# Strip 0 of 576 tokens, batch 1's x by token, and other places for the loads of batches 1, 2 and 3

## The chip, the cores and the metric

The kernel runs on one core of a Trainium2 chip. The metric is the device time of one execution in microseconds (us), as the median of several runs. One further execution was recorded by the hardware profiler; times of single steps below are from that one, counted from the start of its span.

The engines have short names in the profile: PE is TensorE (PEld is its weight load), DVE is VectorE, ACT is ScalarE, POOL is GpSimd, SP is SyncE. L161 is line 161 of the kernel.

## The reference

Linear attention with a norm over each head, and then a bilinear feed-forward layer:

```python
# q, k, v: (8 batches, 8 heads, 576 tokens, 64)
kv = np.einsum('bhsd,bhse->bhde', k, v)
out = np.einsum('bhsd,bhde->bhse', q, kv)
rms = np.sqrt(np.mean(out * out, axis=-1, keepdims=True) + 1e-06)
attn = out / rms * g_norm
# x: (8 * 576 = 4608 tokens, 8 * 64 = 512)
x = attn.transpose(0, 2, 1, 3).reshape(4608, 512)
a = x @ w_a          # 512 -> 1536
b = x @ w_b          # 512 -> 1536
y = (a * b) @ w_out  # 1536 -> 512, float32
```

## The kernel before

All products are taken in bf16 and summed in PSUM, which has eight banks of 512 fp32 columns. `xt` holds x transposed (features on partitions, four chunks of 128, and 4608 tokens along the columns).

**Strips.** The feed-forward layer goes over the tokens in nine strips of 512. In a strip, a `Unit` takes one chunk `fc` of 128 of the 1536 hidden features: four products with `wa_t` (L371), a copy to SBUF by ACT (L373), four products with `wb_t`, and a multiplication by DVE into `abt` (L377). After twelve units follow four output groups (`ffn_o`, L434) of 128 tokens: twelve products with `wo_t` each (`o_mm`), a copy out of PSUM by DVE or ACT in turn (`o_out`, L429 and L431) into one of four buffers `o_sb`, and a store by SP. All matrix products of the layer are issued by `product` (L159 to L161), which splits each into two halves of 64 weight columns when `halves[0]` is set; the halves run side by side.

**Batches.** x of a batch has to be there before the strip that holds its tokens. Batch 0 has 576 tokens, so strip 0 lies within it; strip 1 (tokens 512 to 1023) needs batch 1 as well. Batches 0 and 1 (`EARLY`) have their q, k, v loaded by pairs of heads (`load_pair`, L123), and q is transposed by TensorE (`qtr`). x is made by pair: `px` or `x` (L253, with the block-diagonal `kvb`), then products with `ones` (`pss`) to sum the squares, and `pst` (L240). For batch 1 these steps lie between the pieces of strip 0's output groups (L575 to L591).

From batch 2 on, q goes through DRAM: `load_late(b)` (L136) issues on POOL two DMAs of q into `qs_d[b]` and four of k and v (`ktl`, `vtl`, with two buffers each), and `transpose_q(b)` (L153) has SP transpose it into `qT[b % 2]`. From batch 3 on, a small POOL copy from the other `qT` buffer stands ahead of the issues, so that POOL waits there until the batch before is transposed. `kv` (L170) makes k^T v of all heads. Then x is made by token in five chunks (four of 128 tokens and one of 64): `tx` (L286) multiplies qT and kv into banks 4 to 7, the bank `lent` and bank `O` = 3; ACT squares (`tsq`), DVE sums (`tss`), ACT takes the reciprocal root and POOL multiplies it with g (`trs`), DVE scales to bf16 in `x_tok`, and SP transposes that into `xt` (`txt`).

**Order.** The schedule is by hand: every engine runs its instructions in the order of the program text. In the loop over strips 1 to 7 (L632) each strip has slots n = 0 to 15, twelve units and four output groups. `slot(A, s, n)` (L601) says what of batch s + 1 is done after which unit or group: `k0` is the slot of k^T v, `x0` that of `tx`, and the steps of the chunks follow at distances from `x0`. A half slot lies in the middle of a unit or group. Where `transpose_q` and `load_late` stand is at L644 to L649.

**Loads at the start.** POOL issues, in this order: batch 0's pairs, the weights `wa_t` and `wb_t` in slices of 256 columns (two `fc`), the twelve rows of `wo_t`, batch 1's pairs, and `load_late(2)`.

Of the kernel before, what the change touches and what calls it, by code (L numbers as in the profile page):

```python
# [15 lines left out]
def kernel(  # L16
# [28 lines left out]

    pool = ctx.enter_context(tc.tile_pool(name="sb", bufs=1))
# [21 lines left out]
    kvs = [sb([128, NP, D], BF16, f"kvs{i}") for i in range(2)]  # L68

    kvb = sb([128, NP, 128], BF16, "kvb")  # L70
    xt = sb([128, KC, n_tok], BF16, "xt")
    abt = [[sb([128, STRIP], BF16, f"ab{i}_{f}") for f in range(FC)] for i in range(2)]
# [36 lines left out]
    O = 3  # L109
# [26 lines left out]
    def load_late(b):  # L136
        if b > EARLY:

            nc.gpsimd.tensor_copy(gate, qT[(b - 1) % 2][0:1, 0, 0:1])  # L139
        d = qs_d[b].rearrange("t (h d) -> t h d", h=H)  # L140
        for hs in (slice(0, NP), slice(NP, H)):
            nc.gpsimd.dma_start(out=d[:, hs, :], in_=q[b, hs].rearrange("h t d -> t h d"))  # L142
        n = 128 * LC
        for t, src in ((ktl[b % 2], k), (vtl[b % 2], v)):
            nc.gpsimd.dma_start(  # L145
                out=t[:, :, 0:LC, :],
                in_=src[b, :, 0:n].rearrange("h (t c) d -> t h c d", c=LC),
            )
            nc.gpsimd.dma_start(
                out=t[0 : S - n, :, LC, :], in_=src[b, :, n:].rearrange("h t d -> t h d")  # L150
            )
# [12 lines left out]
    class Attn:  # L164
# [20 lines left out]

        def kv_out(self, ps, src):
            for j in range(2):
                r = slice(j * D, (j + 1) * D)
                nc.scalar.copy(kvb[r, ps, r], src[r])
# [63 lines left out]
        def x(self, p, i0):  # L253
            for h in range(2):
                product(
                    P[:, i0 + h, 0:HF],
                    kvb[:, p, :],
                    self.qT[:, p, h * HF : (h + 1) * HF],
                    start=True,
                    stop=True,  # L260
                )


# [22 lines left out]
        def tx(self, lent):  # L286
            self.lent = lent
            for c in range(LC + 1):
                t0, _ = self.rows(c)
                for p in range(NP):  # L290
                    for j, (i, c0) in enumerate(self.place(c)):
                        r = slice(j * D, (j + 1) * D)
                        nc.tensor.matmul(  # L293
                            P[:, i, c0 + p * D : c0 + (p + 1) * D],
                            lhsT=self.qT[r, p, t0 : t0 + 128],
                            rhs=self.kvs[r, p, :],
                            start=True,
                            stop=True,
                        )


            _, r = self.rows(LC)
            for j, (i, _) in enumerate(self.place(LC)):
                nc.scalar.copy(
                    x_last[r, j], P[r, i, 0 : STRIP // 2].rearrange("t (p d) -> t p d", p=NP)
                )
# [13 lines left out]
        def trs(self, c):  # L320
            _, r = self.rows(c)
            n = r.stop - r.start
# [7 lines left out]
            nc.gpsimd.tensor_mul(  # L330
# [17 lines left out]
    class Unit:  # L348
        n = 0

        def __init__(self, s, fc, a, b):
            self.s, self.fc, self.a, self.b = s, fc, P[:, a, :], P[:, b, :]
            self.t = a_sb[Unit.n % 4]
            Unit.n += 1

        def mm(self, w, kcs):
            t0 = self.s * STRIP
            for kc in kcs:
                product(
                    self.a if w is wa_t else self.b,  # L360
                    w[:, kc, self.fc * 128 : (self.fc + 1) * 128],
                    xt[:, kc, t0 : t0 + STRIP],
                    start=(kc == KORD[0]),
                    stop=(kc == KORD[-1]),
                )
# [5 lines left out]
        def part_a(self, kcs=KORD):  # L371
            self.mm(wa_t, kcs)
            nc.scalar.copy(self.t, self.a)  # L373

        def part_b(self, kcs=KORD):
            self.mm(wb_t, kcs)
            nc.vector.tensor_mul(abt[self.s % 2][self.fc], self.b, self.t)  # L377

        def rest(self, kcs=KORD):
            self.part_a(kcs)  # L380
            self.part_b(kcs)
# [7 lines left out]
    def ffn_ab(s, fc, between=None):  # L389
# [4 lines left out]
        u.b = P[:, ab_bank(), :]  # L394
# [19 lines left out]
    def o_mm(s, g, i, fcs, e0=0, e1=d_model):  # L414
        for fc in fcs:
            product(
                P[:, i, e0:e1],
                abt[s % 2][fc][:, g * 128 : (g + 1) * 128],
# [48 lines left out]
    nc.vector.memset(kvb, 0.0)  # L467
# [10 lines left out]
    for i in range(1, d_ff // WC):  # L478
        load_ab(i * WC, (i + 1) * WC)
    for i in range(FC):  # L480
        load_o(i)
    for p in range(NP):
        load_pair(1, p)
    load_late(2)
# [70 lines left out]
    u1.part_b((2, 3))  # L555

# [6 lines left out]
    for fc in range(4, FC):  # L563
        ffn_ab(0, fc)
# [3 lines left out]
    h1, h2 = range(0, FC // 2), range(FC // 2, FC)  # L568

    nc.sync.dma_start(out=gate_d, in_=vt[1][0:1, H - 1, EC - 1, D - 1 : D])  # L570
    nc.sync.dma_start(out=g_all, in_=g_norm.partition_broadcast(128))
    transpose_q(2)
    ffn_o(0, 0, X[0])
    pieces = [(1, h1), (1, h2), (2, h1), (2, h2), (3, h1), (3, h2)]
    for n, (g, fcs) in enumerate(pieces):  # L575

        halves[0] = n > 0
        o_mm(0, g, O, fcs)
        if fcs is h2:
            o_out(0, g, O)  # L580
        if 0 <= n - 2 < NP:
            A.pss(n - 2, SS)
            A.pst(n - 2, X[n % 2])
        if 0 <= n - 1 < NP:
            A.x(n - 1, X[(n - 1) % 2])
            A.psq(n - 1, X[(n - 1) % 2])
        if n < NP:
            A.qtr(n, 2)
            A.kv1(n, 2)
            A.kv_out(n, P[:, 2, STRIP - D :])  # L590
            A.qtr_out(n, 2)  # L591
    u0 = Unit(1, 0, 2, 3)
    u1 = Unit(1, 1, 4, 5)
    u0.first((0, 1, 2))
    u1.first((0, 1, 2))
    u0.rest((3,))
    u1.rest((3,))
# [3 lines left out]
    def slot(A, s, n):  # L601

        kb = P[:, 7, :].rearrange("q (b p e) -> q b p e", b=2, e=D)
        if s == 1:
            k0, xs = 5, (6.5, 8, 9.5, 11, 12.5)
        else:
            k0, x0 = {2: (2, 3.5), 3: (4, 5.5), 4: (0, 1.5), 5: (4, 5.5), 6: (0, 1.5)}[s]
            xs = tuple(x0 + x for x in (0, 1.5, 2.5, 4, 5))

        k0, x0 = {1: (5, 6.5), 2: (1, 2.5), 3: (4, 5.5), 4: (0, 0.5), 5: (4, 5.5), 6: (0, 0.5)}[s]  # L610
# [9 lines left out]
        if m == 0:  # L620
            A.tx(ab_bank())
        for c in range(LC + 1):
            if m == 1.5 * c:
                A.tsq(c)
            if m == (1, 2, 4, 5, 7)[c]:
                A.tss(c)
            if m == (1, 2, 4, 5, 7)[c] + 0.5:
                A.trs(c)
            if m == (1, 2, 4, 5, 7)[c] + 1.5:
                A.txt(c)  # L630

    for s in range(1, N_STRIP - 1):  # L632
        b = s + 1
        A = Attn(b) if b < B else None
        for n in range(FC + 4):
# [5 lines left out]
            if A:  # L641
                slot(A, s, n)

            if s == 1 and n == 3:  # L644
                load_late(3)
            if b + 1 < B and n == (12, 4, 8, 5, 8)[s - 1]:
                transpose_q(b + 1)
            if b + 2 < B and n == (14, 10, 14, 8)[s - 1]:
                load_late(b + 2)  # L649
# [47 lines left out]
```

## Time and profile before

| | us |
|---|---|
| median of 3 runs | 312.36 |
| lowest and highest | 312.31, 312.39 |
| the profiled execution's own time | 312.61 |
| its span | 310.8 |
| strip 0's first product to its first output product | 14.1 to 35.15 |
| strip 0's output groups with batch 1's attention | 35.15 to 49.96 |
| strip 1, units and output groups | 49.96 to 82.75 |
| one `load_late`, issue of batch 3's six DMAs on POOL | 62.39 to 68.79 |

The times of the stages are read from TensorE's and POOL's timelines: a start time, a duration, the engine and line, the operation with what it writes and reads, and how often. The span is what the profiler saw of the core; the 1.8 us around it belong to the execution's time. TensorE's clock was granted in full (1.00) over the whole span. The groups by line and form give, per instruction, 691 ns for DVE's product of 128x512, 586 ns for ACT's copy of the same size, about 680 ns for DVE's sums and scalings by token, 1046 ns for POOL's product by token, and about 2.6 us from issue to landing for SP's transpose of a chunk of x.

### The profile page before, as it was taken

How to read it: one execution, taken by the hardware profiler on the slowest of the kernel's cores; microseconds unless marked ns; L12 is line 12 of the kernel's file. 1: busy time of each engine (PE TensorE's matmuls, PEld its weight loads, DVE VectorE, ACT ScalarE, POOL GpSimd, SP SyncE). 2: the span in 40 equal slices, each digit the busy share in tenths (PEclk: the TensorE clock that was granted, in tenths of full speed). 3: DMA queues.
4: the chain of work that ended last, by engine and by line, in shares of the span. 5: the costliest groups of instructions: out<-in, count | busy, mean ns of one | idle time of the engine just before them, and what ended most of it. 6: DMA issues, size and time to landing. Idle time of an engine off the chain costs nothing.

```text
span 310.8 us, 6542 instructions
## 1 busy us (share of the span) xinstructions
PE 304.3 (98%) x2684; PEld 157.6 (51%) x2701; DVE 140.6 (45%) x235; ACT 117.0 (38%) x231; POOL 101.3 (33%) x123
## 2 busy tenths in 40 slices
PE   7899999999999999999999999999999999999996
PEld 3444476655555555555555555444444444444444
DVE  4544335458248603484386123752782143214321
ACT  3743255354255313551564034632651233123310
POOL 8954991093274630043646300221240000000000
PEclk9999999999999999999999999999999999999999
DMA  8999999999899999047998990073021200030002
GB/s 180 197 196 199 201 188 168 161 169 184 174 137 185 139 174 193 2 84 134 178 177 118 162 188 2 19 160 110 20 51 42 103 1 0 34 103 0 0 36 101
DMA packets 94403, 36.29 MB, mean 117 GB/s; under 512 B 64934, under 2 KB 89894, under 8 KB 94374
## 3 DMA queue, kind: packets, MB, share of 16 engines
q0 software_dynamic: 59120, 18.44, 56.6%
q1 hardware_dynamic: 34786, 16.93, 25.0%
q10 hardware_dynamic: 468, 0.51, 0.6%
q8 instruction: 21, 0.34, 0.5%
q14 instruction: 8, 0.07, 0.1%
HBM read 37.78 MB, written 12.98 MB: 163 GB/s over the span
## 4 chain that ended last, share of the span: by engine, by line
PE 79%; DMA 12%; POOL 7%; issue 1%; ACT 0%; POOLq 0%
PE P L161 77%; DMA wb_t<-in_moe_w_b_dram 6%; DMA vtl<-in_v_dram 4%; DMA wo_t<-in_moe_w_out_dram 2%; PE P L293 1%; PE P L178 1%; POOL vt L119 1%; POOL qt L119 1%; POOL qs L142 1%; POOL kt L119 1%; POOL wa_t L477 0%; POOL wb_t L477 0%; POOL wo_t L134 0%; POOL ktl L145 0%; POOL vtl L145 0%
## 5 line engine op out<-in xcount | busy, mean ns | idle before, releaser
L377 DVE TENSOR_TENSOR ab<-P,asb 128x512 bf16<-128x512 f32 x108 | 74.4, 691 | 103.2 <-PE P L161 99.9
L161 PE MATMUL P<-xt,wb_t 128*64 128x512 bf16 (+1 forms) x641 | 111.4, 379 | 0.2
L161 PE MATMUL P<-xt,wa_t 128*64 128x512 bf16 (+1 forms) x636 | 111.0, 379 | 0.6 <-issue 0.2
L373 ACT CAST asb<-P 128x512 bf16<-128x512 f32 x108 | 63.1, 586 | 89.6 <-PE P L161 89.5
L161 PE MATMUL P<-wo_t,ab 128*64 128x512 bf16 (+3 forms) x673 | 95.5, 371 | 0.3
L161 PEld LDWEIGHTS <-ab 128*64 128x64 bf16 (+1 forms) x678 | 47.5, 106 | 45.0
L161 PEld LDWEIGHTS <-wa_t 128*64 128x64 bf16 (+1 forms) x644 | 46.0, 106 | 46.2 <-issue 0.6
L161 PEld LDWEIGHTS <-wb_t 128*64 128x64 bf16 (+1 forms) x644 | 45.8, 106 | 45.8
L330 POOL TENSOR_TENSOR sqt<-rst,g_all 128x512 f32<-128x512 f32 (+1 forms) x24 | 25.0, 1046 | 83.0 <-ACT rst L323 83.0
L429 ACT COPY osb<-P 128x512 f32<-128x512 f32 x17 | 10.0, 586 | 70.2 <-PE P L161 60.2
L431 DVE COPY osb<-P 128x512 f32<-128x512 f32 x18 | 12.4, 691 | 44.9 <-PE P L161 40.4
L142 POOL DMA_DIRECT2D qs<-in_q_dram x12 | 19.8, 1654 | 0.7 <-issue 0.3
L314 DVE TENSOR_REDUCE sst<-sqt 128x8 f32<-128x512 f32 (+1 forms) x24 | 16.3, 680 | 1.7 <-ACT sqt L310 1.5
L339 DVE TENSOR_TENSOR qv<-P,sqt 128x512 bf16<-128x512 f32 x18 | 12.3, 681 | 0.0
L330 POOL TENSOR_TENSOR k_x<-rst,g_all 128x512 f32<-128x512 f32 x6 | 6.3, 1044 | 17.4 <-ACT rst L323 17.4
L323 ACT ACTIVATE rst<-sst,eps_t 128x8 f32<-128x8 f32 (+1 forms) x30 | 9.0, 300 | 7.2 <-DVE sst L314 7.0
L310 ACT ACTIVATE sqt<-P 128x512 f32<-128x512 f32 x18 | 10.5, 585 | 0.1
L243 DVE SCALAR_TENSOR_TENSOR xt<-P,g_col,rs 128x288 bf16<-128x288 f32 x16 | 7.5, 511 | 5.1 <-ACT rs L233 5.1
L134 POOL DMA_DIRECT2D wo_t<-in_moe_w_out_dram x12 | 6.4, 530 | 6.7 <-DMA wb_t<-in_moe_w_b_dram 3.2
L233 ACT ACTIVATE rs<-P,eps_t 128x576 f32<-128x576 f32 (+1 forms) x9 | 6.1, 689 | 3.7 <-PE P L161 3.4
L139 POOL COPY gate<-qT 1x1 bf16<-1x1 bf16 x5 | 0.9, 177 | 18.9 <-DVE kvs L618 14.0
L444 PE MATMUL P<-zeros 128*128 128x512 bf16 x16 | 5.8, 510 | 1.2 <-DVE eps_t L461 1.2
(72 smaller groups left out, 131.7 us busy)
## 6 DMA issues: line engine op xcount, KB each, us to landing
out_dram<-osb SPq DMA_DIRECT2D x23, 256.0 KB, 2.1
qs<-in_q_dram POOLq DMA_DIRECT2D x12, 288.0 KB, 7.5
ktl<-in_k_dram POOLq DMA_DIRECT2D x6, 512.0 KB, 9.6
vtl<-in_v_dram POOLq DMA_DIRECT2D x6, 512.0 KB, 12.2
out_dram<-osb SPq DMA_DIRECT2D x13, 128.0 KB, 2.4
wo_t<-in_moe_w_out_dram POOLq DMA_DIRECT2D x12, 128.0 KB, 6.0
wa_t<-in_moe_w_a_dram POOLq DMA_DIRECT2D x5, 256.0 KB, 8.9
wb_t<-in_moe_w_b_dram POOLq DMA_DIRECT2D x5, 256.0 KB, 9.5
```

The source lines that it names most:

```text
L119: nc.gpsimd.dma_start(out=t[:, hs, :, :], in_=src[b, hs].rearrange("h (t c) d -> t h c d", c=EC))
L142: nc.gpsimd.dma_start(out=d[:, hs, :], in_=q[b, hs].rearrange("h t d -> t h d"))
L161: nc.tensor.matmul(o[r], lhsT=lhsT[:, r], rhs=rhs, **kw)
L310: nc.scalar.activation(sqt[c % 3][r], self.by_head(c)[r], AF.Square)
L314: nc.vector.reduce_sum(sst[c % 3][r], sqt[c % 3][r].rearrange("t j p d -> t (j p) d"), axis=mybir.AxisListType.X,)
L323: nc.scalar.activation(rst[c % 3][r], sst[c % 3][r], AF.Abs_reciprocal_sqrt, bias=eps_t[r], scale=1.0 / D,)
L330: nc.gpsimd.tensor_mul(sqt[c % 3][r].rearrange("t j p d -> t (j p) d"), rst[c % 3][r].unsqueeze(2).to_broadcast([n, H, D]), g_all[r].unsqu ...
L339: nc.vector.tensor_mul(t[r].rearrange("t (p j) d -> t j p d", j=2), self.by_head(c)[r], sqt[c % 3][r])
L373: nc.scalar.copy(self.t, self.a)
L377: nc.vector.tensor_mul(abt[self.s % 2][self.fc], self.b, self.t)
L429: nc.scalar.copy(t, P[:, i, :])
L431: nc.vector.tensor_copy(t, P[:, i, :])
```

## The change

Strip 0 takes all 576 tokens of batch 0: its units run over 448 columns (`CUT`), and `ffn_end` does the last 128 for two `fc` at a time in one bank. Strip 1 keeps 448 columns, and its first two units are cut at column 256. `abt` becomes one buffer of 1024 columns for each `fc`. Batch 1's q, k, v are loaded between the weight slices and ahead of `wo`, and its pairs are taken after units 5, 8, 10 and 11 of strip 0. Its x is made by token at the end of strip 0's units, beside the output groups, three of which run together over the rows of `wo`. Batch 2's load is gated by chunk 3 of batch 1's x; its k^T v moves to slot 9 and its `tx` to slot 10 of strip 1. Batch 3's q is loaded at slot 8 and its k and v at slot 15 of strip 1; its k^T v moves to slot 3 of strip 2. Batch 4's load moves from slot 14 of strip 1 to slot 2 of strip 2.

```diff
     def load_late(b):
-        if b > EARLY:
-            nc.gpsimd.tensor_copy(gate, qT[(b - 1) % 2][0:1, 0, 0:1])
+        nc.gpsimd.tensor_copy(gate, qT[(b - 1) % 2][0:1, 0, 0:1])
+        load_late_q(b)
+        load_late_kv(b)
...
+    def ffn_end(fc, i):
+        n = S - CUT
+        t = a_sb[Unit.n % 4][:, 0 : 2 * n]
+        Unit.n += 1
+        for m, w in enumerate((wa_t, wb_t)):
+            for j in range(2):
+                for kc in KORD:
+                    product(
+                        P[:, i, (2 * m + j) * n : (2 * m + j + 1) * n],
+                        w[:, kc, (fc + j) * 128 : (fc + j + 1) * 128],
+                        xt[:, kc, CUT:S],
+                        start=(kc == KORD[0]),
+                        stop=(kc == KORD[-1]),
+                    )
+        nc.scalar.copy(t, P[:, i, 0 : 2 * n])
+        for j in range(2):
+            nc.vector.tensor_mul(
+                abt[fc + j][:, CUT:S],
+                P[:, i, (2 + j) * n : (3 + j) * n],
+                t[:, j * n : (j + 1) * n],
+            )
...
-    for i in range(1, d_ff // WC):
-        load_ab(i * WC, (i + 1) * WC)
+    load_ab(WC, 2 * WC)
+    load_ab(2 * WC, 3 * WC)
+    load_pair(1, 0)
+    load_ab(3 * WC, 4 * WC)
+    hs = [slice(2 * p, 2 * p + 2) for p in range(NP)]
+    load_heads(1, qt[1], q, hs[1])
+    load_heads(1, kt[1], k, hs[1])
+    load_ab(4 * WC, 5 * WC)
+    load_heads(1, vt[1], v, hs[1])
+    load_heads(1, qt[1], q, hs[2])
+    load_ab(5 * WC, 6 * WC)
+    load_heads(1, kt[1], k, hs[2])
+    load_heads(1, vt[1], v, hs[2])
+    load_pair(1, 3)
     for i in range(FC):
         load_o(i)
-    for p in range(NP):
-        load_pair(1, p)
-    load_late(2)
...
+    ffn_end(0, 6)
...
+    ffn_end(2, 7)
...
     for fc in range(4, FC):
+        if fc == 9:
+            ab_banks.remove(4)
         ffn_ab(0, fc)
+        if fc in (5, 8, 10, 11):
+            halves[0] = True
+            pair((5, 8, 10, 11).index(fc))
+        if fc % 2:
+            ffn_end(fc - 1, (ab_banks[0] if fc == FC - 1 else 6 + fc // 2 % 2))
+
+    lent = ab_banks[1]
+    A.tx(lent)
+    A.tsq(0)
+    A.last_out(0)
+    A.tsq(1)
+    A.tss(0)
+    A.trs(0)
...
+    A.trsqrt(3)
+    A.txt(2)
+    A.tg(3, nc.vector)
+    A.txt(3)
+    A.tsq(4)
+    A.tss(4)
+    A.trsqrt(4)
+
+    nc.gpsimd.tensor_copy(gate, x_tok[1][0:1, 0, 0, 0:1])
+    load_late_q(2)
+    load_late_kv(2)
+    A.tg(4, nc.gpsimd)
     transpose_q(2)
+
+    three = (ab_banks[2], ab_banks[0], ab_banks[1])
+    for fc in range(FC + 2):
+        for g, i in enumerate(three):
+            f = fc - (0, 0, 2)[g]
+            if 0 <= f < FC:
+                o_mm(0, g, i, (f,))
+                if f == FC - 1:
+                    o_out(0, g, i)
+    ffn_o(0, 3)
+    u0 = Unit(1, 0, 4, 5)
+    u1 = Unit(1, 1, 6, 7)
+    c = 256
+    for u in (u0, u1):
+        u.mm(wa_t, KORD, (0, c))
+        u.mm(wb_t, KORD, (0, c))
+    for u in (u0, u1):
+        u.part_a(KORD, (c, u.n))
+        u.part_b(KORD, (c, u.n))
...
-        k0, x0 = {1: (5, 6.5), 2: (1, 2.5), 3: (4, 5.5), 4: (0, 0.5), 5: (4, 5.5), 6: (0, 0.5)}[s]
+        k0, x0 = {1: (9, 10), 2: (3, 4.5), 3: (5, 6.5), 4: (0, 0.5), 5: (4, 5.5), 6: (0, 0.5)}[s]
...
+        if s == 1:
+            sqs, sums = (0, 1, 2, 2.5, 4), (0.5, 1.5, 2, 3.5, 4.5)
+            rss, outs = (0.5, 1.5, 2, 3.5, 4.5), (2, 2.5, 3, 4, 5)
+        else:
+            sqs, sums = (0, 1.5, 3, 4.5, 6), (1, 2, 4, 5, 7)
+            rss, outs = (1.5, 2.5, 4.5, 5.5, 7.5), (2.5, 3.5, 5.5, 6.5, 10 if s == 2 else 8.5)
...
-            if s == 1 and n == 3:
-                load_late(3)
-            if b + 1 < B and n == (12, 4, 8, 5, 8)[s - 1]:
-                transpose_q(b + 1)
-            if b + 2 < B and n == (14, 10, 14, 8)[s - 1]:
-                load_late(b + 2)
+            if s == 1:
+                if n == 4:
+                    Attn(1).txt(LC)
+                elif n == 8:
+                    nc.gpsimd.tensor_copy(gate, qT[0][0:1, 0, 0:1])
+                    load_late_q(3)
+                elif n == 14:
+                    transpose_q(3)
+                elif n == 15:
+                    load_late_kv(3)
+            elif s == 2:
+                if n == 2:
+                    load_late(4)
+                elif n == 6:
+                    transpose_q(4)
+                elif n == 10:
+                    load_late(5)
...
```

## The prediction

> **What bounds the kernel now.** I read the page's busy shares first, then the chain that ended last, then TensorE's timeline around the strip 0 / strip 1 border, and last POOL's and SP's timelines.
>
> ```profile
> PE 304.3 (98%) x2684; PEld 157.6 (51%) x2701; DVE 140.6 (45%) x235; ACT 117.0 (38%) x231; POOL 101.3 (33%) x123
> ```
>
> TensorE is busy for 98% of the span; nothing else passes half. The chain shows where something other than TensorE ended last, and TensorE's price:
>
> ```profile
> 47.20 13.45 DMA vtl<-in_v_dram
> 60.65 0.04 issue
> 60.69 0.69 PE P L178 x32
> ...
> 261.80 0.05 issue
> 261.85 10.74 PE P L161 x49
> ```
>
> The reader is to see two things. Batch 2's v lands at 60.65 and is used at once: the only transfer after the start-up that TensorE waits for. And later 50 products of 512 columns take 10.79 us, 0.2158 us each, with no hole. So the time is the sum of TensorE's columns plus its few waits, and the change can gain only by fewer columns, or by removing waits; it loses by any new wait.
>
> TensorE's timeline between the two strips:
>
> ```profile
> 34.29 1.03 PE L161 MATMUL P<-xt,wb_t 128*128 128x512 bf16 x4
> 35.15 4.05 PE L161 MATMUL P<-wo_t,ab 128*128 128x512 bf16 x17
> 39.13 0.45 PE L202 MATMUL P<-ident,qt 96*64 96x96 bf16 x12
> ...
> 43.31 0.44 PE L161 MATMUL P<-sq,ones 128*64 128x288 bf16 x4
> 43.55 0.44 PE L161 MATMUL P<-qT,kvb 128*64 128x288 bf16 x4
> 43.80 0.45 PE L202 MATMUL P<-ident,qt 96*64 96x96 bf16 x12
> ...
> 49.96 0.84 PE L161 MATMUL P<-xt,wa_t 128*64 128x512 bf16 x6
> ```
>
> From 35.15 to 49.96 is 14.81 us. The 48 output products are 48 x 0.2158 = 10.36, so batch 1's attention and its waits are 4.45 us. Starts lie 0.24-0.25 apart for a transpose group, for the four qT/kvb products and for the four ones products, and about 0.19 for a k/v group: 4 x (0.25 + 0.19 + 0.245 + 0.245) = 3.72. The other 0.73 is waiting, mostly the first two transpose groups (0.47 and 0.49 instead of 0.25), whose q and k had just landed.
>
> **What the Trainium skill says.** "TensorE: Matmul & The Clock Gate", section "Wait — 56ns, not 53.3ns?": a warm matmul of N columns starts N/2.4 GHz + 2.5 ns after the one before. The 0.2158 here agrees at 512 columns. The same page, "Back-to-back issue gap", warns of about 81 ns at 128 columns when a weight load goes with each; the tail here disagrees: 12 products of 256 and 24 of 128 columns fill 2.83 us, which leaves about 63 ns for one of 128. The same page, "Architectural detail", has DVE, ACT and GpSimd as strict FIFOs; the trace agrees (below). "DMA: Bandwidth & Descriptors", "Issuing engines are not separate DMA queues": SP's and POOL's transfers share the same 16 DMA engines. The trace agrees: qT of batch 2, transposed beside k and v loads, landed 11.2 us after its issue (50.54 to 61.74), while batch 3's, alone, took 4.7 (79.86 to 84.53).
>
> **Part by part, on TensorE.**
>
> Strip 0 becomes 448 + 128 columns and strip 1 keeps 448. 192 products go from 512 to 448 columns: by the formula (an estimate) 0.1892 instead of 0.2158, so -5.11 us. The 128 columns come back in six `ffn_end` calls of 16 products: 96 products. Lower bound 56 ns (5.4 us), upper 81 ns (7.8 us); I take 62 ns, near the tail's: +5.9. Cutting strip 1's first two units at column 256 adds 16 starts, +0.04.
>
> Batch 1's by-pair x and its ones products go: 8 x 0.245 = -1.96. The by-token x takes their place: 40 small products, 0.69 us in each later strip (the chain's L293 rows), +0.69. The q transposes and k/v groups only move.
>
> The 0.73 of waiting between the strips goes if batch 1's pairs land in time. So does the 0.27 at batch 2's k/v group (1.07 us against 0.80 for batch 3's), unless it comes back. Sum: -5.11 + 5.9 + 0.04 - 1.96 + 0.69 - 1.0 = -1.44 us.
>
> **Loads at the start.** POOL issues a new load when the eighth before it has landed (the order of the waits shows it), so its waits date the landings:
>
> ```profile
> 20.32 0.54 POOL L134 DMA_DIRECT2D wo_t<-in_moe_w_out_dram  x1 [0.60 <-DMA wa_t<-in_moe_w_a_dram]
> 21.66 0.54 POOL L134 DMA_DIRECT2D wo_t<-in_moe_w_out_dram  x1 [0.80 <-DMA wb_t<-in_moe_w_b_dram]
> ```
>
> One 256 KB slice lands each 1.34 us; the slice pair of fc 4-5 is complete at 21.6. A q/k/v pair load of 144 KB costs about 0.70 (batch 1's twelve land from 37.8 to 46.2), a `wo` row 0.68. In the new order the slice pairs of fc 6, 8, 10 land at 26.4, 30.5, 34.6, the last q/k/v at 38.1, `wo` from 38.8 to 46.2. TensorE, with a unit at 1.51, an `ffn_end` at 1.0 and a pair at 0.45, needs them at about 27.6, 31.6, 36.0, 39.0 and from 40.9 (last row 47.6). Each is in time by 1 to 2 us. I take no wait; the upper bound is about 1 us, if this mixture lands 5% slower.
>
> **Batch 1's chain by token.** It starts at about 40.2. ACT's squares (0.59), DVE's sums (0.68), POOL's products (1.05) and DVE's scaling (0.68) finish chunk 3 near 48.1; its transpose lands (2.6, SP issuing one per 1.25) by 51. TensorE covers this with 48 output products and the first 256 columns of two units, until 53: hidden, with 2 us to spare. One small wait is new: output group 1 uses the bank of the last `ffn_end`, which DVE reads until 41.3: +0.25.
>
> **Batch 2's load** now waits for chunk 3's token copy at about 48.3, instead of starting at 41.3. Behind it on POOL stands only chunk 4's product. Batch 3's in this trace took from 62.39 to 78.8 (16.4 us); batch 2's with its transpose beside it 10.1 from q's landing (50.5) to v's. For the new one that gives 65 to 67.6. Its k/v group, moved from slot 5 to 9, is reached at 66.7. I add +0.3, between 0 and 1. Turning q ahead of the stores changes nothing in SP's order: here too the transpose at 50.54 stands before the stores at 57.77, and strip 0's four output buffers are not needed again before about 73. So far -0.9.
>
> **Batch 3's k and v: the step that decides.** They are now loaded at slot 15 of strip 1, apart from q (slot 8), and used after slot 3 of strip 2. On POOL they stand behind batch 2's last token product (chunk 4), in a FIFO. Let U be the start of batch 2's by-token x. TensorE ends unit 11 at U + 2.2 and the output groups 12 to 15 at 4.8, 7.4, 10.0, 12.6 (2.59 each). DVE is in order: it copies group 14 out from 10.0 to 10.7, scales chunk 3 when POOL's product is there (to about 11.9), sums chunk 4 (to 12.6); ACT takes the root (0.3), POOL multiplies (1.05) until about U + 14.1. Only then do the four issues start, and they take 3.2 us:
>
> ```profile
> 65.63 0.90 POOL L145 DMA_DIRECT2D ktl<-in_k_dram  x1
> 66.52 0.70 POOL L149 DMA_DIRECT2D ktl<-in_k_dram  x1
> 67.19 0.91 POOL L145 DMA_DIRECT2D vtl<-in_v_dram  x1
> 68.07 0.72 POOL L149 DMA_DIRECT2D vtl<-in_v_dram  x1
> ```
>
> ```profile
> DMA to landing us min/median/max: 10.4/10.6/10.8
> ```
>
> The last line (from issue to landing, batch 3's v) puts v's end at 78.8; its q landed at 71.0 (64.0 + 7.0). So k and v, queued right behind q, took 7.8 us; for batch 4 8.2, for batch 2 10.1, both with a q transpose beside them. The new load has one too (batch 3's, issued near U + 13) and the stores of groups 14 and 15. I take 8.5 plus 0.9 for the first issue: landing at U + 14.1 + 9.4 = U + 23.5. TensorE wants them after four units of strip 2: 12.6 + 4 x 1.726 = U + 19.5. That is a wait of 4.0 us. Lower bound 1.8 (1.15 MB at 190 GB/s, the page's best slices, is 6.1, plus the first issue and 0.3); upper 6.0 (10.1, an issue, 0.4 of lateness on POOL). Nothing hides it: every product after it is TensorE's and follows in order.
>
> Against the profiled run's own 312.61: -0.9 + 4.0 = 315.7. The median shown is 0.25 lower: 315.5.
>
> **Rivals.**
> 1. *The late k and v of batch 3* (60%): 315.5, own range 313.3 to 317.5.
> 2. *More waits follow* (17%). The gates chain the loads: batch 4's waits for batch 3's transposed q, batch 5's for batch 4's, and k/v of both are used at slot 5 of strip 3. With a transpose at 9.6 to 11.2 instead of 4.7, batch 5's v lands at U + 58 to 61 against a need of U + 55.4 plus the wait before: up to 1.6 more. And a TensorE that stands 4 us may drop its clock (the skill's same page, "What's actually happening", has half clock after an idle window of about 3.4 us; the only cold stretch here is the start, ten products in 4.05 us): about 1.7 more. For it: both clocks and gates are tight. Against it: the earlier wait gives the later loads time. 317.3 to 319.
> 3. *Faster* (23%): batch 3's k and v land in time. This needs a landing within 5.4 us of the first issue; then only the -0.9 to -1.4 stands, 311.0 to 311.5. With a landing at 6.3 the kernel ties, and later than that it loses. For it: no q is ahead in POOL's queue, and fewer packets are in flight. Against it: the issues alone take 3.2.
> 4. *`ffn_end` is weight-load bound* at 81 ns: +1.9, 317.4 with rival 1; it lies inside the range.
>
> **How the numbers follow.** This kernel's measurement tells apart about 0.2%, 0.62 us. Rival 3 gives faster 0.18 and 0.05 within; rivals 1 and 2 give slower 0.77. The range, 311.4 to 318.6, leaves out the lower part of rival 3 and the top of rival 2. The likeliest's own range is given above.
>
> **What would show it.** A k/v group (L178) in strip 2 that starts late, with a hole of about 4 us before it and v's DMA in the chain of waits; strip 2 starting about 1 us earlier than its 82.75; `ffn_end` groups at 0.9 to 1.1 us; POOL's k/v issues after the last token product of batch 2. I am wrong if strip 2 shows no such hole (then rival 3), or if strip 0 itself has holes at a weight slice or at `wo`.

## The result, and the profile after

| | before | after |
|---|---|---|
| median, us | 312.38 | 322.26 |
| lowest and highest, us | 312.31, 312.44 | 322.14, 323.15 |
| the profiled execution's own time, us | 312.61 | 322.27 |
| its span, us | 310.8 | 320.1 |

The change makes the kernel slower: the ratio is 1.0323, with a 95% interval of 1.0304 to 1.0341. That is 9.9 us more, where 3.1 were predicted. In several kernels below the waits, and with them TensorE's clock, differ from one execution to the next; a ratio leaves out the executions that lie more than 1.5% above the fastest of their kernel, so it can stand apart from a median over all of them.

The page of the changed kernel, busy time by engine, with share of the span and number of instructions:

```profile
PE 306.2 (96%) x2953; PEld 163.4 (51%) x2967; DVE 145.6 (45%) x249; ACT 117.9 (37%) x237; POOL 105.8 (33%) x128
```

TensorE was busy for 304.3 us and is now busy for 306.2. Its idle time, the span less that, grew from 6.5 to 13.9 us: most of the loss is waiting. Where it waits, the chain that ended last tells (start, duration, what):

```profile
82.98 1.04 POOL sqt L328
84.02 0.90 POOL ktl L151
84.92 0.67 POOL ktl L155
85.59 10.87 DMA vtl<-in_v_dram
96.45 0.04 issue
96.50 1.49 PE P L184 x25
```

This is the place that the prediction named: POOL multiplies batch 2's last chunk, then issues k and v of batch 3, and v lands at 96.45. Before, the row of this kind was batch 2's v, which landed at 60.65 just in time. TensorE's timeline around it:

```profile
82.47 1.05 PE L167 MATMUL P<-xt,wa_t 128*64 128x512 bf16 x8 [0.67 <-issue]
...
88.51 1.06 PE L167 MATMUL P<-xt,wb_t 128*64 128x512 bf16 x8
96.50 1.49 PE L184 MATMUL P<-vtl,ktl 128*64 128x64 bf16 x40 [6.93 <-DMA vtl<-in_v_dram]
97.74 1.95 PE L167 MATMUL P<-xt,wa_t 128*64 128x512 bf16 x8
99.43 1.90 PE L167 MATMUL P<-xt,wb_t 128*64 128x512 bf16 x8
101.13 1.05 PE L167 MATMUL P<-xt,wa_t 128*64 128x512 bf16 x8
```

Three things are to be seen. Strip 2 begins at 82.47 instead of 82.75. After its fourth unit the k/v group was due near 89.37 (88.51 and four pairs of products at 0.2158), so TensorE loses 7.13 us; the 6.93 of the row counts from the modelled end of the last product, 89.57. And what follows runs at half speed: 1.24 us instead of 0.63 for the k/v group, 3.39 instead of 1.73 for the next unit. The stretches of one microsecond show the clock (window, length, busy time of PE, PEld, DVE, ACT, POOL with counts; then TensorE's clock, the DMA share, GB/s):

```profile
93.00:94.00 1.00, 0.00 (x0) 0.00 (x0) 0.00 (x0) 0.00 (x0) 1.00 (x1) 1.00 1.49 196
94.00:95.00 1.00, 0.00 (x0) 0.00 (x0) 0.00 (x0) 0.00 (x0) 1.00 (x2) 0.65 1.72 180
95.00:96.00 1.00, 0.00 (x0) 0.00 (x0) 0.00 (x0) 0.00 (x0) 1.00 (x1) 0.50 1.36 94
...
101.00:102.00 1.00, 1.00 (x10) 0.41 (x6) 0.57 (x1) 0.00 (x0) 0.00 (x0) 0.94 1.37 184
```

A share of 0.65 means full clock for 0.3 us of that slice, so the clock fell at 94.3, 4.7 us after that end, and came back near 101.1.

The whole loss of the profiled execution (322.27 - 312.61 = 9.66 us) then is: start of strip 2 -0.28, the hole +7.13, the half clock +2.27 (0.61 and 1.66), the time outside the span +0.36 (322.27 - 320.1 = 2.17 instead of 1.81). Together 9.48; 0.2 us are spread over the rest.

### The profile page after: what moved, and what is told of

It is laid out like the page before. It is cut to its first block, busy times and chain, and to the rows that moved or that the text cites. A ratio compares the mean times of both kernels' runs of the same rounds, so it can differ in the third digit from the quotient of the medians.

```text
span 320.1 us, 7120 instructions
## 1 busy us (share of the span) xinstructions
PE 306.2 (96%) x2953; PEld 163.4 (51%) x2967; DVE 145.6 (45%) x249; ACT 117.9 (37%) x237; POOL 105.8 (33%) x128
## 2 busy tenths in 40 slices
DMA packets 96869, 36.91 MB, mean 115 GB/s; under 512 B 67398, under 2 KB 92358, under 8 KB 96838
## 4 chain that ended last, share of the span: by engine, by line
PE 89%; DMA 5%; POOL 1%; DVE 1%; ACT 1%; issue 1%; ACTq 0%; POOLq 0%
PE P L167 84%; DMA vtl<-in_v_dram 3%; PE P L184 2%; DMA qv<-in_v_dram 2%; PE P L283 2%; PE P L203 1%; POOL sqt L328 1%; DVE sst L305 1%; PE P L217 0%; DVE qv L337 0%; ACT sq L226 0%; POOL k_x L328 0%; DVE xt L244 0%; ACT rst L317 0%; POOL ktl L151 0%
## 5 line engine op out<-in xcount | busy, mean ns | idle before, releaser
L379 DVE TENSOR_TENSOR ab<-P,asb 128x512 bf16<-128x512 f32 (+1 forms) x108 | 72.9, 676 | 102.4 <-PE P L167 96.0
L167 PE MATMUL P<-xt,wa_t 128*64 128x512 bf16 (+7 forms) x758 | 113.3, 355 | 1.1 <-issue 0.7
L167 PE MATMUL P<-xt,wb_t 128*64 128x512 bf16 (+7 forms) x761 | 113.3, 355 | 0.2
L375 ACT CAST asb<-P 128x512 bf16<-128x512 f32 (+1 forms) x108 | 61.9, 574 | 94.8 <-PE P L167 94.5
L167 PEld LDWEIGHTS <-wa_t 128*64 128x64 bf16 (+1 forms) x764 | 49.7, 107 | 44.2 <-issue 2.6
L167 PEld LDWEIGHTS <-wb_t 128*64 128x64 bf16 (+1 forms) x764 | 50.1, 107 | 43.2 <-issue 0.8
L328 POOL TENSOR_TENSOR sqt<-rst,g_all 128x512 f32<-128x512 f32 (+1 forms) x27 | 28.1, 1041 | 87.2 <-ACT rst L317 87.1
L184 PE MATMUL P<-vtl,ktl 128*64 128x64 bf16 x240 | 5.2, 203 | 6.9 <-DMA vtl<-in_v_dram 6.9
L184 PEld LDWEIGHTS <-ktl 128*64 128x64 bf16 x240 | 5.0, 119 | 8.0 <-DMA ktl<-in_k_dram 3.7
L283 PEld LDWEIGHTS <-qT 64*128 64x128 bf16 x280 | 4.5, 95 | 2.5 <-issue 2.4
```

The lines of the kernel that those rows point to most:

```text
L167: nc.tensor.matmul(o[r], lhsT=lhsT[:, r], rhs=rhs, **kw)
L184: nc.tensor.matmul(o[j * D : (j + 1) * D, :], lhsT=kk[0:n, 2 * p + j, c, :], rhs=vv[0:n, 2 * p + j, c, :], start=(c == 0), stop=(c == len( ...
L283: nc.tensor.matmul(P[:, i, c0 + p * D : c0 + (p + 1) * D], lhsT=self.qT[r, p, t0 : t0 + 128], rhs=self.kvs[r, p, :], start=True, stop=True,)
L328: eng.tensor_mul(sqt[c % 3][r].rearrange("t j p d -> t (j p) d"), rst[c % 3][r].unsqueeze(2).to_broadcast([n, H, D]), g_all[r].unsqueeze(1 ...
L379: nc.vector.tensor_mul(abt[self.fc][:, self.c0 : self.c0 + self.n], self.b, self.t)
```

## The experiments

**Issue k and v earlier.** The simplest theory: they come late because POOL reaches them late. So the first kernel issues them ahead of batch 2's token products.

```diff
+                elif n == 5:
+                    load_late_kv(3)
                 elif n == 8:
...
-                elif n == 15:
-                    load_late_kv(3)
```

> Batch 3's k and v are loaded at slot 5 of strip 1 instead of slot 15; all else as changed. Theory (the late issue on POOL made the whole loss, directly as a hole of 7.1 us and through the clock that it dropped, 2.3 us): no hole at the k/v group of strip 2, clock full throughout, 322.3 - 9.4 = 312.9 us, within 0.4. Rival (the DMA engines are short of time in strips 1 and 2, wherever the load stands): the load delays batch 2's k and v or its q transpose instead, a hole of 2 us or more opens in strip 1, and the time stays above 315.

Measured: 320.56 (317.34 to 323.63), ratio 1.0178 (1.0161 to 1.0194). In the profiled execution (322.45 us) the hole at batch 3's k/v group is gone, but 4.1 us of waits stand at the groups of batches 4 and 5, 1.9 at batch 2's qT in strip 1, and 1.2 at the start of strip 2. The chain of waits there:

```profile
99.80 8.97 DMA qT<-qs
108.77 0.05 issue
108.82 0.18 POOL gate L139
...
114.80 18.58 DMA vtl<-in_v_dram
133.38 0.04 issue
133.42 1.07 PE P L184 x17
```

Batch 4's q took 9.0 us to be transposed, the gate for batch 5's load opened behind it, and batch 5's v needed 18.6. So the theory that only the place on POOL counts falls; the rival, that the DMA engines are short of time, held in the time, though its largest wait lies in strip 3 and the one in strip 1 is a little under the 2 us it named.

**A little earlier; the transpose out of the way.** In one kernel `load_late_kv(3)` moves from slot 15 to slot 14, in the other `transpose_q(3)` from slot 14 to slot 13.

```diff
-                elif n == 14:
+                elif n == 13:
                     transpose_q(3)
```

> Batch 3's k and v are loaded at slot 14, ahead of the last token product on POOL instead of behind it. Theory (POOL's FIFO place counts): the issue starts at about 81.1 instead of 84.0 and v lands 2.9 us earlier; the hole shrinks from 7.1 to about 4.2, and with less idle time the clock may not drop: 317.1 to 319.4 us. Rival (the landing is set by the DMA engines, not by the issue): v still lands at 96 or so, 322 us.

> SP's transpose of batch 3's q moves from slot 14 to slot 13, so that it runs ahead of the k and v load instead of beside it; the load's issue stays at 84.0. Theory that the transpose beside the load is what made the load take 12.5 us instead of my 9.4: v lands about 3 us earlier, hole 4 us, 317 to 319.5 us. Rival (the load is slow by itself): v lands at 96 as before, 322 us.

Measured: 326.23 (324.48 to 327.24), ratio 1.0434 (1.0409 to 1.046), and 323.57 (321.96 to 325.61), ratio 1.0358 (1.032 to 1.0396). With slot 14 the issue came 3 us sooner, at 80.94, and v still landed at 96.2; batch 3's transposed q took 13.6 us, and TensorE waited 8.6 us for v in four places, two of them in strip 3. With the transpose ahead, its gate let batch 4's q go at 87.46, beside k and v, and v landed at 98.05. So at this place an issue 3 us earlier bought no earlier landing; what the transpose alone does is not shown here, since batch 4's q took its place.

**Is it only company in the queues?** Here nothing of batch 4 is issued until batch 3's k^T v is made, and the transpose stands at slot 13, so k and v of batch 3 have POOL's queue to themselves; SP's stores and two transposes of x still run beside them.

```diff
                 if n == 2:
-                    load_late(4)
+                if n == 3:
+                    nc.gpsimd.tensor_copy(gate, kvs[1][0:1, 0, 0:1])
+                    load_late(4)
```

> As transpose3_slot13, and batch 4's load waits until batch 3's k^T v has been copied out, so that nothing else of POOL's is in flight beside batch 3's k and v, and SP's q transpose is over. Theory that other transfers beside it (the transpose in the changed kernel, batch 4's q in transpose3_slot13) make the load slow: v lands 9 to 10 us after the first issue instead of 12.5 and 14. Rival (the load is slow by itself): 12 us or more. The time is not the point: batch 4's load comes late, so a hole in strip 3 is to be expected, 320 us or more.

Measured: 330.11 (329.46 to 332.62), ratio 1.0579 (1.0549 to 1.0609). Its chain:

```profile
84.04 0.90 POOL ktl L151
84.94 0.67 POOL ktl L155
85.61 12.38 DMA vtl<-in_v_dram
97.99 0.04 issue
98.03 1.28 PE P L184 x22
```

They land no sooner: 14.0 us after the first issue. Such a load is slow even with nothing behind it in its queue. TensorE waits 8.5 us for them. Batch 4's load comes later too, and another 3.3 us of waits stand in two places at the k/v groups of batches 4 and 5 in strip 3.

**The clock.** Thirty products of zeros ahead of batch 3's k/v group fill the hole without using anything of DMA.

```diff
+            if s == 2:
+                dummy(30, 5)
```

> 30 products of zeros (6.5 us at full clock) are put ahead of the k/v group in strip 2, into the hole; they add work to TensorE and leave the load as it is. Theory (after 5 us of idleness the clock fell to half, and 2.3 us of the loss are the k/v group and the next unit at half clock): the hole is filled, the clock stays full, 322.3 - 2.3 = 320.0 us. Rival (the slow instructions after the hole are slow for another reason, the DMA traffic or late operands): 322 us, or more.

Measured: 320.62 (319.85 to 321.08), ratio 1.0258 (1.0245 to 1.0272), 1.6 us less than the change by the medians, where 2.3 were expected. In the profiled execution it is 1.8, although strip 2 begins 0.37 us later there (82.84). Its page shows the granted clock in 40 slices, full throughout:

```profile
PEclk9999999999999999999999999999999999999999
```

In the changed kernel the same row has an 8 and a 6 where strip 2 stands still and starts again:

```profile
PEclk9999999999986999999999999999999999999999
```

So the clock's part is shown, and it is the smaller part.

**Batch 3's whole load at slot 8.** k and v go right behind q.

> Batch 3's k and v follow its q at once at slot 8 of strip 1, as one load, as the kernel before has it. Revised theory (the loads of batches 2 to 5 are one chain of gates and transfers; it starts 7.7 us later than before, and its last user, the k/v group of batches 4 and 5 in strip 3, only 1.7 us later): no hole at batch 3's k/v group, but the hole appears at slot 5 of strip 3, 3 to 5 us, with or without a clock drop: 316 to 320 us. First theory (the late issue of batch 3's k and v was the whole loss): 312.9 us.

Measured: 319.92 (319.05 to 321.31), ratio 1.0243 (1.0221 to 1.0264). No wait at batch 3's k and v, none at batches 4 and 5. The time lies in the range that was expected, but not for the reason that was given: the hole was to come in strip 3, and it is strip 2 itself that starts late:

```profile
78.65 3.19 PE L167 MATMUL P<-wo_t,ab 128*64 128x512 bf16 x28
88.35 1.92 PE L167 MATMUL P<-xt,wa_t 128*64 128x512 bf16 x8 [6.52 <-issue]
```

SP's transposes of x between 74 and 84, from issue to landing, in this kernel:

```profile
DMA to landing us min/median/max: 6.5/8.1/9.2
```

and in the changed kernel (74 to 82), where no load is under way:

```profile
DMA to landing us min/median/max: 2.4/2.5/2.5
```

This is the second half of the answer: x by token needs transposes on the critical path, and these were short here only while no load ran. The quiet stretch in which batch 3's k and v are not loaded is what x of batch 2 lives on.

**Two attempts to make room.** Both have batch 3's load at slot 8. The first adds later slots in strip 3, where k and v of batches 4 and 5 are used (`k0, x0` = 9, 10 with strip 1's distances, batch 6's load at slot 15). The second also takes the small waits away: chunk 2 transposed at `x0` + 2.5 instead of 3, and the second output group of strip 0 one row behind the first.

```diff
-            f = fc - (0, 0, 2)[g]
+            f = fc - (0, 1, 2)[g]
```

> As load3_slot8, and the k/v group of batches 4 and 5 moves from slot 5 to slot 9 of strip 3, with batch 4's x at slot 10 in the spacing of strip 1, and batch 6's load from slot 14 to 15. Revised theory (the chain of loads needs about 4 us more room at its last user, and all else of the change costs nothing): no hole anywhere in strips 2 and 3, 311.8 to 312.8 us. Rival (there is another loss further on, in strips 4 to 8): above 314 us.

> As load3_slot8_kv45_slot9, and two small waits taken out: chunk 2 of x is scaled and transposed ahead of output group 13's store in SP's queue (0.7 us before strip 2), and output group 1 of strip 0 runs one row of wo later, so that it doesn't wait for its bank (0.2 us). Theory: 0.5 to 0.9 us less than load3_slot8_kv45_slot9, about 311.4 us, faster than the kernel before by 0.3%. Rival (the waits only move): the same as load3_slot8_kv45_slot9.

Measured: 320.74 (319.01 to 323.47), ratio 1.0277 (1.0242 to 1.0312), and 320.13 (317.55 to 322.42), ratio 1.0208 (1.018 to 1.0237). Both expectations missed: the hole before strip 2 stayed, at 6.9 and 6.4 us. Later uses of k and v don't help: it is the transposes that are late now.

**Batch 2's load earlier.** Perhaps everything is late because batch 2's load is gated by batch 1's chunk 3 and starts at 49.0 instead of 41.3. One kernel takes that gate out of the kernel above (batch 3's load at slot 8), one issues batch 2's load ahead of batch 1's x by token.

```diff
-    nc.gpsimd.tensor_copy(gate, x_tok[1][0:1, 0, 0, 0:1])
     load_late_q(2)
     load_late_kv(2)
```

> As load3_slot8, without the gate ahead of batch 2's load, which then follows chunk 2's product on POOL at about 46.1 instead of 49.0. Theory (the chain of loads is late as a whole, and the transposes of x that strip 2 needs collide with its second part): all loads come 2.9 us earlier, the 6.5 us hole at the start of strip 2 shrinks by about that, and the time falls by 2.5 to 4.5 us from 319.9 to 315.4 to 317.4, unless batch 1's own transposes now land late. Rival (the collision is there whenever a load runs, the start doesn't matter): 319 to 321 us.

> The changed kernel with batch 2's load issued at the start of batch 1's by-token chain, ahead of its products on POOL, with no gate. Theory (the transposes of x by token need a quiet stretch of the DMA engines and POOL's early products, and the change pays for that stretch with a later load): the products start 6.5 us later and the transposes land beside the load, so a new hole of 5 to 9 us opens at the start of strip 1 and the hole in strip 2 stays, since batch 3's k and v are issued behind batch 2's last product as before: 327 to 332 us. Rival (the quiet stretch isn't needed): 322 us or less.

Measured: 320.94 (320.13 to 321.35), ratio 1.0268 (1.0254 to 1.0281), and 332.70 (331.44 to 332.99), ratio 1.0639 (1.0623 to 1.0655). Without the gate the load starts at 46.18; the hole before strip 2 shrinks to 0.7 us, a new one of 3.2 us opens in strip 1, and 2.0 us stand at batches 4 and 5. With the load ahead, strip 1 waits for batch 1's x:

```profile
60.21 1.06 PE L167 MATMUL P<-xt,wa_t 128*64 128x256 bf16 x8 [8.47 <-DMA xt<-qv]
```

and batch 3's k and v cost another 6.7. Here the theory held but for 0.7 us at the top of its range; for the kernel without the gate the rival did, as the time did not fall. The hole moves; it does not close.

**All of it together.** No gate for batch 2, batch 3's load at slot 8, strip 2's first two units cut at column 256 as strip 1's are, and the small waits removed.

> As load3_slot8_load2_ungated, with strip 2's first two units cut at column 256 like strip 1's, chunk 2 ahead of group 13's store, and output group 1 of strip 0 one row of wo later. Theory: 1.7 us more room before chunks 1 and 2 are needed, and 0.9 us of small waits less: 313 to 315 us, still not faster than before. Rival (the kernel can be made faster than before within this order): below 312 us.

Measured: 322.88 (321.69 to 327.57), ratio 1.0312 (1.0297 to 1.0327). A miss: in the profiled execution (325.41 us) 5.2 us of wait in strip 1, 2.0 at strip 2, 2.5 at batches 4 and 5.

**The loads taken out.** Is TensorE's own work as short as predicted, if two of the loads are left out? The two kernels here leave out k and v of batches 3 and 5, so they do not compute the reference; only their time is of use. The first let the groups of batches 3 and 5 read what lay in the buffers of batches 2 and 4.

> The k and v of batches 3 and 5 are not loaded at all; their k/v groups multiply the buffers of batches 2 and 4 instead, so TensorE's work is the same and 2.3 MB of transfers are gone. Theory (TensorE's own work and order in the changed kernel are no slower than before; the whole loss is the loads): no hole in strips 2 and 3, clock full, 312.9 us, the same as before within 0.3%. Rival (part of the 9.9 us is in TensorE's work or in the by-token chain): 315 us or more.

Measured: 330.99 (328.92 to 333.12), ratio 1.0594 (1.0559 to 1.0629), and it tells nothing: in the order of the program batch 3's group then stood behind batch 4's load into the same buffer, and waited 14.1 us for that. The second kernel takes batch 1's buffers, which nothing writes again (48 products a group instead of 40).

```diff
-            if self.b < EARLY:
-                kk, vv, rows = kt[self.b], vt[self.b], [EP] * EC
+            if self.b in (0, 1, 3, 5):
+                i = min(self.b, 1)
+                kk, vv, rows = kt[i], vt[i], [EP] * EC
```

> The changed kernel, with the k and v of batches 3 and 5 not loaded at all; their k/v groups multiply batch 1's buffers (48 products for a pair instead of 40, 0.3 us more in all). Theory (TensorE's own work and order in the changed kernel are no slower than before; the whole loss is the loads): no hole in strips 2 and 3, clock full, 313.0 us, the same as before within 0.4%. Rival (part of the 9.9 us is in TensorE's work or in the by-token chain): 315 us or more.

Measured: 313.37 (312.89 to 314.64), ratio 1.003 (1.0017 to 1.0043). Its timeline at the places that matter:

```profile
54.18 0.52 PE L167 MATMUL P<-xt,wa_t 128*64 128x192 bf16 x8 [0.84 <-DMA xt<-qv]
...
83.25 1.05 PE L167 MATMUL P<-xt,wa_t 128*64 128x512 bf16 x8 [0.62 <-issue]
```

Two small waits are left once the start-up is over. With two of the loads gone the change costs 1 us instead of 10: the loss is in the loads, not in TensorE's products. The two waits (1.5), the extra products (0.3) and 0.3 us outside the span, less the 0.95 that TensorE's sum saves (see the next section), make about this 1 us.

**The same delay in the kernel before.** If a late start of batch 2's load is enough, the kernel before must suffer from it as well. There `load_late(2)` and its transpose move behind strip 0's output pieces, gated by the last pair of batch 1's `qT`.

```diff
+    nc.gpsimd.tensor_copy(gate, qT[1][0:1, NP - 1, 0:1])
+    load_late(2)
+    transpose_q(2)
```

> The kernel before, with batch 2's load gated by batch 1's last q pair, so that it starts at about 48.5 instead of 41.3, and with its q transpose behind it; nothing else is changed. Theory (in the kernel before too the load chain has no room, so a start 7 us later is paid in full): a hole of 5 to 8 us before batch 2's k/v group in strip 1, with up to 2.3 us of half clock behind it: 317.5 to 322.5 us. Rival (the later start is taken up by slack, the loss comes from elsewhere in the change): 314 us or less.

Measured: 319.59 (318.94 to 319.88), ratio 1.0226 (1.0212 to 1.0239). TensorE's timeline there:

```profile
64.09 0.42 PE L178 MATMUL P<-vtl,ktl 128*64 128x64 bf16 x8 [3.64 <-DMA vtl<-in_v_dram]
65.22 1.06 PE L178 MATMUL P<-vtl,ktl 128*64 128x64 bf16 x32 [0.71 <-DMA vtl<-in_v_dram]
66.05 1.94 PE L161 MATMUL P<-xt,wa_t 128*64 128x512 bf16 x8
```

Started at 48.34, v landed at 65.18. A load 7 us later costs 7.2 us in a kernel that has none of the other parts of the change: a hole of 4.35 us, a little less than expected, and half clock after it.

## Why the prediction was right on the sign and wrong on the size

**TensorE's sum up to strip 2: right.** Predicted -0.9 us. Measured -0.28, and this holds a wait of 0.67 us that was not in the sum: without it -0.95. The bound on `ffn_end` was 56 to 81 ns a product; measured are the lower 56 (the next product starts 0.90 us after 16 of them):

```profile
17.91 0.61 PE L167 MATMUL P<-xt,wa_t 128*128 128x128 bf16 x8
18.36 0.61 PE L167 MATMUL P<-xt,wb_t 128*128 128x128 bf16 x8
18.81 1.49 PE L167 MATMUL P<-xt,wa_t 128*128 128x448 bf16 x7
```

This is the 55.8 ns that the Trainium skill ("TensorE: Matmul & The Clock Gate", "Wait — 56ns, not 53.3ns?") gives; rival 4's 81 ns fell. But the match to 0.05 us is partly luck. `ffn_end` was put 0.5 too high (6 x 0.90 = 5.4 instead of 5.9), and the +0.3 at batch 2's k/v group did not come; about 0.6 of small gaps in strip 0, which the sum left out, made up for most of it (its products fill 25.4 of the 26.3 us from 14.11 to 40.41; before, 20.7 of 21.05). The loads at the start came in time, as argued. Batch 2's k/v group was forecast at 66.7 and began at 66.81, without the +0.3. Its `tx` came at 69.05; this is the prediction's U, for which its sum gives 69.15 (66.7 and 0.3, a k/v group of 0.63, a unit of 1.51).

**The wait that was missed.** The prediction said of SP's queue only that the early transpose changed nothing. It did not follow batch 2's chunks there. SP's queue, in the changed kernel:

```profile
78.66 0.99 SPq L430 DMA_DIRECT2D out_dram<-osb  x2
79.75 1.23 SPq L341 DMA_TRANSPOSE xt<-qv  x1
81.07 1.00 SPq L430 DMA_DIRECT2D out_dram<-osb  x2
```

Chunk 2 of batch 2 is issued behind the stores of group 13, at 79.75, and 2.5 us of landing put strip 2's first product at 82.47: +0.67.

**The step that failed: the landing of batch 3's k and v.** The prediction put POOL's issue at U + 14.1 and TensorE's need at U + 19.5; measured are 83.96 and 89.37, U + 14.9 and U + 20.3, so the two errors cancel. It put the landing 9.4 us after the first issue, "8.5 plus 0.9"; it came 12.5 after, at 96.45. The 8.5 was won by taking q's landing from v's: q and k/v were thought to stand in line, so that without q ahead k and v would be done sooner. The runs say otherwise. For v of batch 3 the trace of the changed kernel answers the view that the prediction showed:

```profile
DMA to landing us min/median/max: 10.4/10.6/10.9
```

Before it was 10.4/10.6/10.8, with q in front. The transpose of q that ran beside it now and not before does not explain this: with it issued 2.3 us earlier, at 81.16, and nothing else on POOL's queue (the kernel with k and v alone) v took 12.0. So v's own time from issue to landing was the number to take, unshortened. v's first issue came 1.6 us after k's; with 10.8, the longest of batch 3's before, the prediction's own sum would have been U + 14.1 + 1.6 + 10.8 = U + 26.5, a wait of 7.0 instead of 4.0. The upper bound of 6.0 failed for the same reason: its 10.1 was again a difference of landings. The other batches' v took 11.0 to 13.4 us in the kernel before (medians of the same view), so 10.8 was the low end; with 13.4 the sum gives a wait of 9.6.

**The clock** stood in rival 2, at about 1.7 us; it came, at 2.27. With 7 us instead of 4 it belonged into the main case. The Trainium skill (same page, "What's actually happening") says half clock after an idle window of about 3.4 us. The 4.7 us here agree; but in the kernel before with its late load 3.0 were enough (idle from 60.45, down at 63.44), and in the kernel without the gate for batch 2 the clock fell at 58.2, when TensorE had been at work again for 1.2 us behind a wait of 3.2. So a wait need not last 3.4 us.

In sum, the difference of 6.6 us between forecast and profiled execution is 3.1 of landing, 2.3 of clock, 0.6 at strip 2's start, 0.36 outside the span, and the 0.2 that is spread over the rest.

**The other half of rival 2,** gates that chain the loads, did not show in the changed kernel, since the long hole gave the later loads time, as the argument against it said. It appeared as soon as that hole was taken away (k and v at slot 5).

**What the prediction did not see at all** is why no single move mends this. Before, the loads of batches 2 and 3 ran on with hardly a pause (v landed at 60.65, the next issue came at 62.39); here is the kernel before, two stretches in the columns given above:

```profile
41.00:61.00 20.00, 19.90 (x280) 14.01 (x276) 9.31 (x18) 10.51 (x22) 6.64 (x7) 1.00 1.61 157
61.00:80.00 19.00, 19.00 (x233) 10.47 (x227) 11.10 (x18) 8.80 (x19) 11.77 (x12) 1.00 1.41 187
```

and the changed kernel, where the same bytes have to pass:

```profile
46.00:52.00 6.00, 6.00 (x62) 3.31 (x60) 4.61 (x8) 1.97 (x5) 3.21 (x4) 1.00 0.61 100
52.00:74.00 22.00, 22.00 (x328) 14.43 (x324) 9.84 (x16) 9.04 (x19) 9.26 (x11) 1.00 1.56 181
74.00:86.00 12.00, 11.33 (x108) 6.21 (x104) 7.21 (x11) 4.96 (x10) 5.92 (x7) 1.00 0.67 131
```

The shares are to be compared with each other only, as they pass 1. From 46 to 52 and from 74 to 86 the share is less than half of what it was: these are the stretches in which x of batches 1 and 2 is made by token and transposed. They are needed, for with a load inside them the transposes take 6.5 to 9.2 us instead of 2.5. Before, batch 1's x went through TensorE and needed no DMA, so batch 2's load could run underneath. And batch 2's x did lie beside batch 3's load, with transposes as slow as that; SP's view between 70 and 78, kernel before:

```profile
DMA to landing us min/median/max: 6.8/7.0/7.2
```

But the two that this line counts were issued at 70.6 and 72.3, ten us and more ahead of strip 2; in the changed kernel batch 2's chunks are issued from 76.0 on. By the prediction's sum, x of batch 1 by token saved 1.3 us of TensorE's products (1.96 less 0.69). For that, batch 2's load starts 7.7 us later, and the time found no place elsewhere: every arrangement tried had its hole at another place, and none was faster than the kernel before.

**What stays open.** Why v needs 10.6 to 12 us from its issue with the queue empty but for k: many packets are small (67,398 of the page's 96,869 are under 512 bytes), but nothing here varied their size, and no run took SP's transfers away. So is the source of the 0.36 us outside the span (2.1 to 2.2 us lie there in every kernel made from the changed one, 1.7 and 1.8 in the two of the kernel before), and whether another form of the transposes of x, or loads in smaller parts between them, would let this schedule win the 1 us that TensorE's sum offers.

## What to carry to other kernels

Take a load's latency from its own issue to its landing, and don't shorten it by the transfer in front unless a run shows that the two wait for each other. When work moves from an engine to a DMA, count the quiet time that its DMAs need as time taken from the loads, and follow each load on to its use. A wait on TensorE can cost more than its length. In these traces the clock fell to half with every wait of 3.2 us or more, and with three pairs of shorter ones close together (2.2 and 0.9 us, 2.4 and 0.9, 1.5 and 1.0); a single wait of 2.0 us and a pair of 1.2 and 0.8 left it full.

## What the runs showed of the hardware that was not expected

- v's issue-to-landing time did not shrink without q in front: 10.6 us for batch 3 behind q, 10.6 without q, 12.0 with nothing else on POOL's queue (medians of its parts). Behind q it was 10.6 to 13.4 over the batches of the kernel before.
- A transpose of an x chunk landed in 2.4 to 2.5 us in a quiet stretch, and in 6.5 to 9.2 us beside a load; a transpose of a whole q took 4.7 us alone, 9.0 and 13.6 us beside loads.
- The clock came back 4.6 us after TensorE had started again (96.50 to 101.1), 3.3 in the kernel with k and v alone and 5.2 in that with batch 3's load at slot 8, and filler products of zeros kept it from falling at all.
- The clock changed in steps of 3.41 us. Between the start-up and the last product the traces hold 17 stretches of half clock: four of 3.4 us, eleven of 6.8, one of 10.2 and one of 17.1. In the four kernels with two of them the second began 13, 13, 14 and 23 times 3.41 us after the first (138.90 after 94.52 with k and v alone, 136.88 after 58.38 with all together). So what a wait costs depends also on where it falls between these steps.
